# The global part of a joined attention product as eight 64x64 matmuls into free columns of the score banks, with new order lists

## The chip, the cores and the metric

The kernel runs on one core of a Trainium2 chip. The core has a matmul engine (PE; its weight loads are listed apart as PEld), a vector engine (DVE), a scalar engine (ACT), GpSimd (POOL) and a queue that issues transfers (SP). Each engine takes its instructions in the order in which the program lists them, and waits at semaphores for the others. PE writes into PSUM, a memory of eight banks with 512 fp32 columns on each of 128 partitions; DVE and ACT read results from there. The metric is the device time of one launch in microseconds.

## What is computed

Eight batches and eight heads of an attention with a local window, followed by a two-layer network on all 8 x 544 rows:

```python
k_all = concatenate([k_g, k_l]); v_all = concatenate([v_g, v_l])      # 32 global rows, 512 local ones; head size 64
out_g = sm(scale * q_g @ k_all.T) @ v_all                             # global rows see everything
s_ll  = where(abs(i - j) <= 32, scale * q_l @ k_l.T, -1e9)            # a local row sees 32 rows on each side
s_lg  = scale * q_l @ k_g.T                                           # and all 32 global rows
out_l = sm(concatenate([s_lg, s_ll])) @ concatenate([v_g, v_l])
h = x @ w_in                                                          # x: heads side by side, 4352 x 512; w_in 512 x 2048
out = (h * clip(h + 3, 0, 6) / 6) @ w_out                             # w_out 2048 x 512
```

## The kernel before

**A local step.** The 512 local rows of a batch are four blocks of 128, so there are 32 local steps (batch, block), written (b, j). A step sees, for each head, 128 columns of banded local scores and 32 columns of global scores. `local_step` lays out its operations:

- The scores, on PE (line 677, the inner function `pe`): 64x64 tiles of the array, 16 matmuls of 128 columns and 16 of 32 columns. Their result is the tile `scored` (named `s` in the profile): four whole PSUM banks, each with the 160 columns of two heads (columns 0 to 319). There is one such set, the ring "S".
- Eight reductions on DVE (line 703), one a head: mask added, maximum taken, the result written to `sm` in SBUF. When all eight are done the set is given back.
- Eight exponentials on ACT (line 714), then reciprocals and scalings on DVE (lines 725, 730, 736), and a transpose into `et`; from batch 2 on by a transfer (line 759), before that by PE.
- The product with V (`av`, lines 763 to 771): 16 matmuls of 128x64 shape and 64 columns for the local part (line 768), and four of 128x128 shape and 128 columns for the global part (line 771). For the latter `vgz` holds the 32 global rows of V of four heads on 128 partitions, for each pair of heads with zeros where another head's columns stand. The result is one bank, the tile `a`, the ring "A".
- A copy of that result to `xt` in fp16, the network's input (`xa` in `done`, lines 400 on ACT or 402 on DVE, which are the helper `copy`).

**Joined steps.** From the seventh step on (`JOIN = 6`) the scores of a step and the product of the step two before are one operation on PE: `both` issues the scores and then `av` of the older step. There are 26 of these, steps (1,2) to (7,3). Four products before and two at the end run alone (`alone`).

**The global rows.** `global_steps` makes, once a batch, the scores of the 32 global rows of all heads with the same four banks (line 817), two maxima on DVE (832), two exponentials on ACT (840) and scalings (847, 848), a transpose to `eg`, and a product with V into the tile `a` (876).

**The network.** `first` (line 899) multiplies `xt` with a part of `w_in` into one of three banks `m`; ACT makes the clipped part (906) and DVE the product (910) into `gs`. `second` (922) multiplies `gs` with `w_out` in four quarters of four matmuls; ACT or DVE copies the result to `ot` (400, 402), and SP stores it (940). The network of batch b runs among the attention of batch b + 1.

**The order.** All operations are numbered as they are added. `ORDER` holds, for each engine, the list of these numbers in the order in which the engine is to take them; where an operation can go to ACT or DVE (`BOTH`), the list that holds it decides. `Plan.lay` goes through the lists with estimated durations and gives each operation a start and a buffer of its ring; the program is issued over all engines in the order of these starts. At the start 44 idle matmuls are put in between (line 1050). Waits are put in by the framework from the tiles that instructions read and write.

Of the kernel before, what the change touches and what calls it, by code (L numbers as in the profile page):

```python
# [65 lines left out]
    """,  # L66
    "DVE": """
# [242 lines left out]
def kernel(  # L310
# [12 lines left out]
    nc = tc.nc  # L323
    P = 128
# [763 lines left out]
```

## Time and profile before

| | |
|---|---|
| median of 3 runs | 324.29 us (323.80 to 324.64) |
| profiled execution | 324.56 us, of it 322.8 us from its first instruction to its last |
| granted PE clock | 1.0 throughout |
| busy: PE, DVE, ACT, POOL | 312.4, 261.0, 237.8, 121.4 us |
| L922 and L899, the network's products | 126.1 us in 560 matmuls, 119.1 us in 704 |
| L703, the reductions | 68.6 us in 256 |
| L771, the global part | 128 matmuls, 12.7 us busy, the lone steps included |

Rows of the profile name line, engine, operation and tiles as `out<-in`. Matmuls are pipelined: the next starts long before the one ahead has ended, so the cost of a matmul on PE is the distance between starts and not its duration. A merged row of the timeline gives the start of its first instruction and the length up to the end of its last.

### The profile page before, as it was taken

To read this page: it belongs to the slowest core of one execution; us is meant where nothing else is said; L and a number is where in the kernel's file an instruction comes from. 1 tells how busy PE (TensorE), PEld (TensorE's weight loads), DVE (VectorE), ACT (ScalarE), POOL (GpSimd) and SP (SyncE) were. 2 spreads that over 40 slices of the span, in tenths; PEclk is the share of its full clock that TensorE was granted. 3 is DMA by queue.
4 is the path that set the end of the run, shared out by engine and by line. 5 is a ranking of instruction groups with operands and counts; after the bars stand their busy time and mean duration, and the time that the engine had idled before them with its cause. 6 is when DMAs were issued, how large, how long until landed. Compare 5 with 4: busy or idle time off the path is not lost.

```text
span 322.8 us, 9551 instructions
## 1 busy us (share of the span) xinstructions
PE 312.4 (97%) x3554; PEld 178.3 (55%) x3554; DVE 261.0 (81%) x959; ACT 237.8 (74%) x761; POOL 121.4 (38%) x167
## 2 busy tenths in 40 slices
PE   8988999999999999999999999999999999999995
PEld 4557885657855544545444554445444445655443
DVE  4999999899998799789988998889978976476201
ACT  3699999999977897688976897687878834465200
POOL 7958857969190492364334350320000000000000
PEclk9999999999999999999999999999999999999999
DMA  9999999999999999999999999899313055200132
GB/s 162 154 193 172 178 214 156 160 147 150 198 162 201 166 151 171 151 260 183 128 201 215 164 137 179 197 176 206 83 32 68 1 142 156 65 2 0 49 115 99
DMA packets 178863, 46.35 MB, mean 144 GB/s; under 512 B 169344, under 2 KB 173696, under 8 KB 178816
## 3 DMA queue, kind: packets, MB, share of 16 engines
q0 software_dynamic: 108800, 17.28, 76.7%
q1 hardware_dynamic: 70016, 28.45, 44.6%
q8 instruction: 28, 0.46, 0.6%
q14 instruction: 19, 0.16, 0.2%
HBM read 35.65 MB, written 8.91 MB: 138 GB/s over the span
## 4 chain that ended last, share of the span: by engine, by line
PE 73%; DVE 10%; DMA 8%; ACT 6%; issue 2%; SPq 0%; POOLq 0%; DVEq 0%; ACTq 0%
PE m L922 31%; PE m L899 29%; PE s L677 3%; DVE sm L703 3%; PE a L768 3%; PE a L771 3%; DMA eg<-pg 2%; DMA et<-pn 2%; ACT sm L714 2%; DVE gs L910 2%; DVE pn L730 2%; PE a L876 1%; DMA out_dram<-ot 1%; ACT t L906 1%; DMA natg<-in_k_g_dram 1%
## 5 line engine op out<-in xcount | busy, mean ns | idle before, releaser
L922 PE MATMUL m<-wout,gs 128*128 128x512 f16 (+1 forms) x560 | 126.1, 373 | 0.0
L899 PE MATMUL m<-xt,win 128*128 128x512 f16 (+2 forms) x704 | 119.1, 321 | 1.1 <-DVE gs L910 0.4
L714 ACT ACTIVATE sm<-sm,stat 128x160 f32<-128x160 f32 x256 | 107.1, 423 | 12.8 <-DVE stat L703 12.1
L910 DVE SCALAR_TENSOR_TENSOR gs<-t,m 128x512 f16<-128x512 f32 x136 | 91.6, 683 | 18.9 <-ACT t L906 17.9
L899 PEld LDWEIGHTS <-win 128*128 128x128 f16 x768 | 69.0, 98 | 48.4 <-issue 2.8
L906 ACT ACTIVATE t<-m 128x512 f32<-128x512 f32 x136 | 79.4, 595 | 19.7 <-PE m L899 18.4
L922 PEld LDWEIGHTS <-gs 128*128 128x128 f16 x560 | 53.3, 98 | 56.3 <-issue 1.4
L703 DVE CUSTOM_DVE_ANT_0 sm<-s,mask 128x160 f32<-128x160 f32 x256 | 68.6, 317 | 3.7 <-PE s L677 3.5
L714 ACT ACTIVATION_READ_ACCUMULATOR sm<-sm,stat 128x1 f32 x256 | 49.6, 194 | 0.0
L730 DVE TENSOR_TENSOR pn<-sm,stat 128x512 f16<-128x512 f32 x64 | 43.3, 685 | 0.8
L479 POOL DMA_DIRECT2D nat<-in_q_l_dram x30 | 27.3, 918 | 40.8 <-DMA qk<-nat 35.5
L479 POOL DMA_DIRECT2D ve<-in_v_l_dram x40 | 33.1, 839 | 10.8 <-PE a L876 10.8
L400 ACT COPY ot<-m 128x512 f32<-128x512 f32 (+1 forms) x23 | 12.9, 565 | 25.1 <-PE m L922 24.2
L400 ACT CAST xt<-a 128x512 f16<-128x512 f32 x29 | 16.9, 583 | 15.2 <-PE a L771 15.0
L479 POOL DMA_DIRECT2D nat<-in_k_l_dram x30 | 27.3, 913 | 0.4 <-DMA wout<-in_moe_w_out_dram 0.4
L479 POOL DMA_DIRECT2D vgz<-in_v_g_dram x28 | 15.7, 569 | 30.9 <-PE a L771 30.8
L703 DVE DVE_READ_ACCUMULATOR2_ANT stat<- 128x1 f32 x256 | 21.1, 82 | 0.0
L677 PEld LDWEIGHTS <-qk 64*64 64x64 f16 x1024 | 13.5, 107 | 12.5 <-issue 11.2
L402 DVE COPY ot<-m 128x512 f32<-128x512 f32 x12 | 8.2, 686 | 14.6 <-PE m L922 13.2
L677 PE MATMUL s<-qk 64*64 64x128 f16 x512 | 16.6, 224 | 1.1 <-DVE stat L703 0.7
L725 DVE RECIPROCAL stat<-stat 128x4 f32<-128x4 f32 x64 | 10.6, 171 | 6.9 <-ACT sm L714 6.3
L677 PE MATMUL s<-gt,qk 64*64 64x32 f16 x512 | 14.5, 176 | 0.0
(77 smaller groups left out, 253.3 us busy)
## 6 DMA issues: line engine op xcount, KB each, us to landing
out_dram<-ot SPq DMA_DIRECT2D x31, 256.0 KB, 3.7
nat<-in_q_l_dram POOLq DMA_DIRECT2D x30, 128.0 KB, 5.6
nat<-in_k_l_dram POOLq DMA_DIRECT2D x30, 128.0 KB, 5.7
st<-ve SPq DMA_DIRECT2D x14, 256.0 KB, 5.1
ve<-in_v_l_dram POOLq DMA_DIRECT2D x24, 128.0 KB, 5.5
win<-in_moe_w_in_dram POOLq DMA_DIRECT2D x4, 512.0 KB, 9.0
wout<-in_moe_w_out_dram POOLq DMA_DIRECT2D x4, 512.0 KB, 9.7
ve<-in_v_l_dram POOLq DMA_DIRECT2D x8, 96.0 KB, 5.1
```

Of the source, the lines that this page charges most:

```text
L400: nc.scalar.copy(out=out, in_=in_)
L479: nc.gpsimd.dma_start(out=dst(op), in_=src)
L677: nc.tensor.matmul(out=out[q, P:KW] if n == G else out[q, 0:P], lhsT=qk[r][rows, 0, p, UQ + j * P + u * QP:UQ + j * P + (u + 1) * QP], rhs ...
L703: nc.vector.tensor_tensor_reduce(out=sm[sm_op.slot][:, h, :], in0=head(psS[s.slot], h), in1=m, scale=-scale, scalar=3.0e38, op0=ALU.add, o ...
L714: nc.scalar.activation(out=sm[sm_op.slot][:, h, :], in_=sm[sm_op.slot][:, h, :], func=EXP, scale=-1.0, bias=stat[stat_op.slot][:, 0, h:h + 1],
L725: nc.vector.reciprocal(out=stat[stat_op.slot][:, 2, h0:h1], in_=stat[stat_op.slot][:, 1, h0:h1])
L730: nc.vector.tensor_tensor(out=pn[pn_op.slot][:, h0:h1, :], in0=sm[sm_op.slot][:, h0:h1, 0:P], in1=stat[stat_op.slot][:, 2, h0:h1].unsqueez ...
L768: nc.tensor.matmul(out=ps[e * D:(e + 1) * D, h // 2, q], lhsT=x[:, j, h * D:(h + 1) * D], rhs=w[:, h, q], start=u == 0 and h < 2, stop=False)
L899: nc.tensor.matmul(out=psM[op.slot][:, i * n:(i + 1) * n], lhsT=w_in_t[:, m, (c + i) * P:(c + i + 1) * P], rhs=x()[:, m, t0:t0 + n], start ...
L906: nc.scalar.activation(out=t1[to.slot], in_=psM[f.slot], func=RELU, bias=0.5, scale=1.0 / 6.0)
L910: nc.vector.scalar_tensor_tensor(out=gs[set_.slot][:, c:c + k, t0:t0 + n], in0=t1[to.slot].rearrange("f (k t) -> f k t", k=k), scalar=1.0, ...
L922: nc.tensor.matmul(out=psM[(f or op).slot][:, a * n:(a + 1) * n], lhsT=gs[set_.slot][:, c, t0:t0 + P], rhs=w_out_t[:, c, a * n:(a + 1) * n ...
```

## The change

For joined steps alone:

1. The result goes into columns 320 to 447 of the four score banks, in place of the tile `a`: bank p gets the pair of heads p. The joined operation asks for the ring "S" only.
2. The global part comes first, right behind the scores, as eight matmuls on 64 rows, 64 columns of the array and 128 columns of data, one for each head; they use the half of `vgz`'s rows and columns in which the head's values and one other head's zeros stand. They start the sums, and the 16 matmuls of the local part add to them.
3. The copy to `xt` reads the score banks. It depends, beside the product, on the last of the eight reductions that the code adds, `trs[-1]`, which is head 7's. The score banks are given back when all eight reductions and the copy are done.
4. The copy is added after the step's exponentials and no longer before its reductions, so it has another number: in step (4,1) it was 1037 and is 1055, and the reductions of heads 0 to 7, which were 1040, 1042, ... 1054, are 1039, 1041, ... 1053.
5. All five order lists are new. The planner's duration of a joined operation is 955 in place of 1080.

```diff
     "PE": """
...
-        1036 975 954 965 868 1141 966 1137 967 968 1145 1153 1063 1149 1157 1161 1165 1173 1169 1091 1177 1181
...
+        17 14 12 40 65 23 21 61 99 63 90 131 93 95 57 163 124 127 399 391 129 156 195 159 403 407 387 161 235
...
+        1036 954 975 965 868 1141 966 1137 967 1145 968 1153 1063 1149 1157 1161 1165 1173 1169 1177 1181 1091
...
     "ACT": """
...
+        1023 1019 1025 1021 1027 1017 1055 963 1050 1048 1052 956 1040 1046 1054 1142 1143 1044 871 1042 872
...
     "DVE": """
...
+        1029 1018 1028 1032 1030 1033 1031 1034 1037 1038 1053 1047 962 1041 1049 1043 1045 1051 976 1039 977
...
-    psS = [scored]
+    psS, spare_s = [scored], scored[:, :, 2 * KW:2 * KW + P]
...
             def both(op):
                 pe(op)
-                before[0](op.slots[1])
-            s = add("PE", 1080, both, deps + before[1], key=key, acq=("S", "A"), rel=before[2], cols=1664, ins=8 * H + AV)
-            before[3](s)
+                before[0](None)
+            s = add("PE", 955, both, deps + before[1], key=key, acq="S", rel=before[2], cols=1408, ins=8 * H + AV + 8)
...
+        if before:
+            before[3](s, trs[-1:])
+            plan.at = "soft", b, j
...
         def av(slot):
-            ps, w = psA[slot].rearrange("d (p q) -> d p q", p=NP), et[et_op.slot]
+            w = et[et_op.slot]
+            ps = psA[slot].rearrange("d (p q) -> d p q", p=NP) if slot is not None else spare_s
+            if slot is None:
+                for p in range(NP):
+                    for e in range(2):
+                        rows, cols = slice(p % 2 * D, p % 2 * D + D), slice(e * D, e * D + D)
+                        nc.tensor.matmul(out=ps[cols, p, :], lhsT=vgz[r][rows, p, cols], rhs=w[rows, H + p // 2, :],
+                                         start=True, stop=False)
             for u, x in enumerate((ve[b % VE], st[r])):
                 for h in range(H):
                     e, q = h % 2, slice(u * QP, (u + 1) * QP)
                     nc.tensor.matmul(out=ps[e * D:(e + 1) * D, h // 2, q], lhsT=x[:, j, h * D:(h + 1) * D], rhs=w[:, h, q],
-                                     start=u == 0 and h < 2, stop=False)
-            for p in range(NP):
+                                     start=slot is not None and u == 0 and h < 2, stop=slot is None and u == 1)
+            for p in range(NP if slot is not None else 0):
                 nc.tensor.matmul(out=ps[:, p, :], lhsT=vgz[r][:, p, :], rhs=w[:, H + p // 2, :], start=False, stop=p == NP - 1)
...
-        def done(v):
+        def done(v, after=()):
...
             def xa(op):
                 copy(op, xt[xt_op[b].slot][:, :, j * P:(j + 1) * P],
-                     psA[v.slots[-1]].rearrange("k (p q) -> k p q", p=NP))
-            xdone[b, j] = [add(BOTH, (470, 610), xa, [v, xt_op[b]], key=key - 0.5, rel=[v])]
+                     spare_s if after else psA[v.slots[-1]].rearrange("k (p q) -> k p q", p=NP))
+            xdone[b, j] = [add(BOTH, (470, 610), xa, [v, xt_op[b], *after], key=key - 0.5, rel=[v])]
```

179 rows, old and new, of the table ORDER are left out of this document.

## The prediction

> **What bounds the kernel now.** I read the first part of the page, then its chain, then one long window, then the waits.
>
> ```profile
> span 322.8 us, 9551 instructions
> PE 312.4 (97%) x3554; PEld 178.3 (55%) x3554; DVE 261.0 (81%) x959; ACT 237.8 (74%) x761; POOL 121.4 (38%) x167
> ...
> PE 73%; DVE 10%; DMA 8%; ACT 6%; issue 2%; SPq 0%; POOLq 0%; DVEq 0%; ACTq 0%
> PE m L922 31%; PE m L899 29%; PE s L677 3%; DVE sm L703 3%; PE a L768 3%; PE a L771 3%; DMA eg<-pg 2%; DMA et<-pn 2%; ACT sm L714 2%; DVE gs L910 2%; DVE pn L730 2%; PE a L876 1%; DMA out_dram<-ot 1%; ACT t L906 1%; DMA natg<-in_k_g_dram 1%
> ```
>
> The matmul engine is busy nearly all the time, and the chain runs mostly through the two large products (L922, L899). The view of busy time by stretch, for the stretch that holds nearly all joined steps:
>
> ```profile
> core 0: us, PE busy (x) PEld busy (x) DVE busy (x) ACT busy (x) POOL busy (x), PEclk, DMA share, GB/s
> 60.00:265.00 205.00, 203.88 (x2325) 109.05 (x2327) 181.92 (x675) 166.33 (x555) 74.57 (x101) 1.00 1.35 154
> ```
>
> Here PE idles 205.00 - 203.88 = 1.1 us, DVE 23.1 us, ACT 38.7 us, at full clock. So work taken from PE is time won, as long as nothing new makes PE wait. DVE is second: its room is 23 us in 24 of the 26 joined steps, about 0.9 us a step.
>
> **What the change takes away.** In a joined step PE makes the scores (L677), then the local part of an older step's product with V (L768), then its global part (L771). One joined step, step (4,0), in the timeline (start, duration, instruction):
>
> ```profile
> 130.10 0.25 PE L677 MATMUL s<-qk 64*64 64x128 f16 x4
> 130.18 0.19 PE L677 MATMUL s<-gt,qk 64*64 64x32 f16 x4
> 130.21 0.23 PE L677 MATMUL s<-qk 64*64 64x128 f16 x4
> 130.27 0.19 PE L677 MATMUL s<-gt,qk 64*64 64x32 f16 x4
> ...
> 130.44 0.19 PE L677 MATMUL s<-gt,qk 64*64 64x32 f16 x4
> ...
> 130.56 0.32 PE L768 MATMUL a<-et,ve 128*64 128x64 f16 x8
> ...
> 130.70 0.32 DVE L703 CUSTOM_DVE_ANT_0 sm<-s,mask 128x160 f32<-128x160 f32 x1
> 130.71 0.29 PE L768 MATMUL a<-et,st 128*64 128x64 f16 x8
> ...
> 130.94 0.40 PE L771 MATMUL a<-et,vgz 128*128 128x128 f16 x4
> ...
> 131.17 4.48 PE L922 MATMUL m<-wout,gs 128*128 128x512 f16 x20
> ...
> 131.37 0.58 ACT L400 CAST xt<-a 128x512 f16<-128x512 f32 x1 [1.43 <-PE a L771]
> ```
>
> The global part costs 131.17 - 130.94 = 0.23 us. It becomes eight 64x64 matmuls of 128 columns, two rounds of four tiles, in the mode that the scores already use. The second such round of the scores takes 130.27 - 130.21 = 0.06 us, the first 130.18 - 130.10 = 0.08. Two rounds: 0.12 (at worst 0.16); won: 0.11 us a step (0.07). There are three changes of tile shape in a step before and after. The eight weight loads replace four larger ones; the scores do 32 in 0.46 us, 0.014 each, so eight need 0.11 and fit under the two rounds. 26 joined steps: **-2.9 us** (bounds -1.8 and -3.0). Nothing covers this on PE, so all of it counts.
>
> The result no longer needs the bank "a", whose only other users are the few lone products and the global rows' product. In the waits no row has PE waiting for a copy out of "a", so freeing it is worth 0 (at most the 1.1 us that PE idles).
>
> **What the change adds.** The product now lies in free columns of the four score banks, in the tile `s`. Three consequences.
>
> First, a reduction (L703) waits for the last matmul that wrote its tile. In the step above it starts at 130.70, just after the last score row (130.44 + 0.19 = 130.63), with L768 still running into another bank. With L768 writing the same tile it can start when that ends: 130.71 + 0.29 = 131.00, plus 0.12 for the two rounds, plus the same 0.07: 131.19, that is **1.09 us after the step's start in place of 0.60**.
>
> Second, the copy to `xt` reads the same banks as the eight reductions. In the row above the copy on ACT runs at 131.37 beside the reductions on DVE. What happens to two engines that read one tile is shown by the global rows' softmax, batch 6, where DVE takes maxima of `s` (L832) and ACT its exponentials (L840):
>
> ```profile
> 234.47 0.72 DVE L832 TENSOR_REDUCE stat<-s 128x1 f32<-128x544 f32 x1 [0.74 <-PE s L817]
> ...
> 235.23 0.15 DVE L834 TENSOR_SCALAR stat<-stat 128x1 f32<-128x1 f32 x1
> 235.30 0.71 DVE L832 TENSOR_REDUCE stat<-s 128x1 f32<-128x544 f32 x1
> 235.51 0.19 ACT L714 ACTIVATION_READ_ACCUMULATOR sm<-sm,stat 128x1 f32 x1
> ...
> 236.11 0.71 ACT L840 ACTIVATE sg<-s,stat 128x544 f32<-128x544 f32 x1 [0.41 <-DVE stat L832]
> ```
>
> Both order lists put the first half of the heads first (1614 before 1622 on DVE, 1616 before 1624 on ACT). That half's bias is ready at 235.23 + 0.15 = 235.38, ACT is free at 235.70, and yet the exponential starts at 236.11, 0.10 after the second maximum ends (235.30 + 0.71 = 236.01), although that one reads the other half's banks. The waits say the same:
>
> ```profile
> ACT xt L400 <- PE a L771: 15.0, 13, 2.4
> ...
> DVE sm L703 <- PE s L677: 3.5, 4, 1.9
> ...
> ACT sg L840 <- DVE stat L832: 1.8, 3, 1.1
> ...
> PE m L899 <- DVE gs L910: 0.4, 2, 0.2
> ```
>
> So two engines' reads of `s` are taken in turn, in the order in which the program issues them. I apply that to the copy: it waits for the reductions issued before it, and those issued behind it wait for the copy. The Trainium skill, "PSUM — Partial Sum Buffer", section "PSUM bank collisions raise a hardware error", has the reason: two engines on one bank and quadrant at once is an error, reads against reads included, so software must keep them apart. By that rule the copy, which touches all four banks, collides with every reduction; the sum is the same as by the row, and no run here shows an unguarded pair.
>
> The new lists are laid out as if only one reduction mattered. The copy depends in the code on `trs[-1]` alone, head 7's. In step (4,1) the DVE list takes that one first (1053 1047 ... 1041 1049 1043 1045 1051 ... 1039), and the ACT list has the copy, 1055, ahead of the step's first exponential. Of the 26 joined copies 19 stay on ACT; head 7's reduction is first or second of its step in 10 of these and third to sixth in 9. The other 7 are on DVE, where before there was one; the output copies on DVE fall from twelve to nine. Behind the copy in the ACT list stand the step's exponentials (L714). The copies' cost, from the view of the tile `xt` and from the page's groups:
>
> ```profile
> L400 ACT CAST xt<-a x29: 562/585/615, 21.9 to 280.3; 128x512 f16<-128x512 f32 x29
> L402 DVE CAST xt<-a x3: 660/682/685, 27.6 to 270.4; 128x512 f16<-128x512 f32 x3
> ```
> ```profile
> L402 DVE COPY ot<-m 128x512 f32<-128x512 f32 x12 | 8.2, 686 | 14.6 <-PE m L922 13.2 <-DMA out_dram<-ot 1.4
> ```
>
> DVE gets 6 x 0.68 - 3 x 0.69 = +2.0 us of work; and where the copy cuts into the reductions DVE stands still for 0.58 and two hand-overs of about 0.07, **0.72 us**. In some ten steps that is 7 us (bounds: none, 0; all nineteen, 13.7). With the late first reduction (0.49 at most, for the steps where DVE was early, about ten: 4 us) DVE loses 11 + 2 = 13 of its 23 us of room. On average it is no bottleneck, but it works in order, and behind a halted reduction stand L910 and L402, for which PE waits with its three `m` banks. I take a sixth of these 13 us as PE wait, **+2** (bounds 0 and 13), nearest to the row in which PE idles 1.1 us with DVE 89% busy.
>
> Third, the score banks are given back only after the copy. There is one set, so the next score operation on PE waits for it. Three places, steps (4,1), (6,0) and (7,0), where the global scores (L817) follow closest; timeline, start of scores, first and last reduction, next use:
>
> ```profile
> 135.58 0.25 PE L677 MATMUL s<-qk 64*64 64x128 f16 x4
> ...
> 136.53 0.32 DVE L703 CUSTOM_DVE_ANT_0 sm<-s,mask 128x160 f32<-128x160 f32 x1
> ...
> 138.48 0.08 DVE L703 DVE_READ_ACCUMULATOR2_ANT stat<- 128x1 f32 x1
> ...
> 139.48 0.21 PE L817 MATMUL s<-gt 64*32 64x32 f16 x8
> ```
> ```profile
> 230.22 0.25 PE L677 MATMUL s<-qk 64*64 64x128 f16 x4
> ...
> 231.70 0.32 DVE L703 CUSTOM_DVE_ANT_0 sm<-s,mask 128x160 f32<-128x160 f32 x1
> ...
> 233.65 0.08 DVE L703 DVE_READ_ACCUMULATOR2_ANT stat<- 128x1 f32 x1
> ...
> 233.97 0.21 PE L817 MATMUL s<-gt 64*32 64x32 f16 x8
> ```
>
> In both lists the same three quarter products of L922 stand between, so PE arrives 233.97 - 230.22 = 3.75 us after the start, in the new kernel 3.64. Eight reductions in a row take 138.56 - 136.53 = 2.03 us. The new hold is 1.09 + 2.03 + 0.72 + 0.07 = 3.91 if DVE is at hand, and 1.48 + 2.03 + 0.79 = 4.30 if it comes as late as at 231.70: PE waits 0.3 to 0.7, taken 0.45, three times: 1.3 us. Six more crossings have little room in the new PE list: (1,3) to (2,0), (2,1) to global 1, (2,3) to global 2, (5,0) to global 4, (7,2) to global 7, and in (7,1) the first L899 of batch 6, which needs that step's copy and comes behind one quarter product: PE is there after 131.17 - 130.10 - 0.11 = 0.96 and four of the twenty matmuls in 4.48, 0.90, that is 1.86, and the copy cannot end before 1.09 + 0.25 + 0.72 = 2.06. I take 0.3 each, between 0 and the 0.7 above: 1.8 us. Together **+3.1 us** (bounds 0 and 6.3).
>
> The moved entries of the POOL and SP lists add and remove no transfer, and the chain gives both queues 0%: 0. The first four entries of the PE list change places too; the chain has the load of `natg` there with 1% of the span: 0, a microsecond either way. The three output copies given to ACT lie in its 38.7 us of room; 0.
>
> **Sum.** -2.9 + 2.0 + 3.1 = +2.2 us. The profiled execution took 324.56 us (322.8 of span and 1.8 around it), 0.27 above the median of 324.29. 324.56 + 2.2 = 326.8, against the median 326.5; I say **326.6 us**.
>
> **Rivals.**
> - *PE's saving comes through.* DVE's room of 0.9 us a step swallows each halt of 0.72 before PE needs the bank, and the banks come back in time because the new lists put the users of `s` further apart where they could, (5,0) to global 4 by one quarter product. For it: the quoted 23 us of room. Against it: the three crossings above, where the list leaves 3.64 for a hold of 3.91. It decides if PE's waits from `s` and `m` stay under 2 us in all. 324.3 - 2.9 + 0.8 = about 322.2. Chance 0.27.
> - *The waits cancel the saving.* Crossings of 1.3 + 0.9 and a DVE effect under 1: within 0.3% (1 us, about what a measurement of this kernel can tell), 323.3 to 325.3. Chance 0.12.
> - *DVE becomes the bound.* The copy is in turn with the reductions in all nineteen steps and each halt reaches PE by way of the `m` banks: 13.7 + 3.1 - 2.9 = +13.9 at most, with half of it reaching PE +7: 331.3. For it: DVE's 89%. Against it: PE waits for L910 0.4 us in all, by the quoted row. Chance 0.17.
> - *The reads aren't kept in turn.* Then copy and reductions overlap, the hold is 1.09 + 2.03 + 0.07 = 3.2 and fits 3.64. The time is the first rival's, and I count it there; the row at 236.11 speaks against it.
>
> **How the numbers follow.** Likeliest: slower by waits for `s`, 326.6, chance 0.44, own range 325.3 to 329.0. With the DVE case 0.61 slower, 0.12 same, 0.27 faster. The range reaches from 321.5 (the saving whole, no new wait: 324.3 - 2.9) to 331.3.
>
> **What would show it.** In the page after: L771 gone or small, L768 with the 64x64 rows added and PE busy time down by about 3 us. A row "DVE sm L703 <- ACT xt" of some microseconds in the waits and "PE s L817" or "PE s L677 <- ACT xt" of 1 to 4 us. First reductions 1.1 us after a step's start, never 0.6. If copies on ACT run beside reductions on DVE in the timeline, the second consequence is wrong; if the global rounds cost over 0.16 us, the saving is; if PE's idle time from 60 to 265 us stays near 1 us, the kernel is faster and the third is wrong.

## The result and the profile after

The changed kernel takes **328.99 us** (median of 5 runs, 328.48 to 330.12); the kernel before, beside it, 323.97 us (5 runs, 323.80 to 324.64). The ratio is 1.0158, 95% interval 1.0135 to 1.0181: slower, as forecast, and 2.4 us above the 326.6 forecast, inside the range. The change itself was forecast at +2.3 us (326.6 - 324.3) and measured at +5.0, over twice as much. The profiled execution took 328.59 us, 4.0 more than that of before.

The first part of the page after, and its chain:

```profile
span 326.8 us, 9756 instructions
PE 311.0 (95%) x3660; PEld 174.0 (53%) x3660; DVE 261.7 (80%) x959; ACT 237.5 (73%) x761; POOL 121.4 (37%) x167
...
PE 46%; DVE 32%; ACT 11%; DMA 6%; issue 3%; SPq 2%; ACTq 0%; DVEq 0%
```

PE's busy time fell by 1.4 us, and the span rose by 4.0. In the chain DVE's share went from 10% to 32%. Lines have moved: the reductions are L702 now, the exponentials L713, the product's rounds L772 and L777, the global scores L826, the network's products L908 and L931.

The stretch from 60 to 265 us of the changed kernel, in the columns of the view of before (PE, PEld, DVE, ACT, POOL, clock, DMA share, GB/s):

```profile
60.00:265.00 205.00, 198.33 (x2382) 103.17 (x2381) 179.41 (x661) 161.48 (x540) 75.36 (x102) 1.00 1.34 155
```

PE idles 205.00 - 198.33 = 6.7 us in place of 1.1, at full clock, and DVE and ACT are busy for less of it as well: all three engines wait for each other more. The waits of the changed kernel (who waits, for whom, total us, how often, longest):

```profile
ACT xt L400 <- DVE stat L702: 13.8, 12, 2.7
DVE sm L702 <- ACT xt L400: 9.4, 16, 0.7
...
PE m L908 <- DVE gs L919: 2.2, 7, 0.7
...
PE s L826 <- DVE stat L702: 1.8, 4, 0.7
DVE sm L702 <- PE s L777: 1.6, 3, 0.8
PE s L677 <- DVE stat L702: 1.2, 4, 0.4
```

The first two rows are new: the copy on ACT waits 13.8 us for reductions on DVE, and the reductions 9.4 us for the copy. Not all of the 13.8 is added waiting: before, ACT's copies to `xt` waited 15.0 us for the product (a row that the prediction shows). Step (4,1), for which the prediction worked out the hold of the banks, in the timeline:

```profile
136.38 0.25 PE L677 MATMUL s<-qk 64*64 64x128 f16 x4
...
136.76 0.28 PE L772 MATMUL s<-et,vgz 64*64 64x128 f16 x8
136.97 0.32 PE L777 MATMUL s<-et,ve 128*64 128x64 f16 x8
...
137.34 2.92 PE L931 MATMUL m<-wout,gs 128*128 128x512 f16 x12
137.46 0.32 DVE L702 CUSTOM_DVE_ANT_0 sm<-s,mask 128x160 f32<-128x160 f32 x1
...
137.95 0.08 DVE L702 DVE_READ_ACCUMULATOR2_ANT stat<- 128x1 f32 x1
138.12 0.59 ACT L400 CAST xt<-s 128x512 f16<-128x512 f32 x1 [2.40 <-DVE stat L702]
...
138.74 0.33 DVE L702 CUSTOM_DVE_ANT_0 sm<-s,mask 128x160 f32<-128x160 f32 x1 [0.71 <-ACT xt L400]
...
140.21 0.08 DVE L702 DVE_READ_ACCUMULATOR2_ANT stat<- 128x1 f32 x1
...
140.35 0.21 PE L826 MATMUL s<-gt 64*32 64x32 f16 x8
```

The joined operation now lasts 137.34 - 136.38 = 0.96 us instead of 1.07. The first reduction comes 1.08 us after the start. Two reductions run, the copy waits for them, the third waits for the copy: it starts 0.79 us later than its place at 137.95. The banks come back at 140.21 + 0.08 = 140.29, 3.91 after the start, and the next user of `s` starts at 140.35.

Where PE's time went is seen in its groups (busy, mean ns of one, idle just before). First before, then after:

```profile
L899 PE MATMUL m<-xt,win 128*128 128x512 f16 (+2 forms) x704 | 119.1, 321 | 1.1 <-DVE gs L910 0.4 <-DVE xt L402 0.3 <-DVE ot L402 0.2
L677 PE MATMUL s<-qk 64*64 64x128 f16 x512 | 16.6, 224 | 1.1 <-DVE stat L703 0.7 <-ACT sg L840 0.2
L817 PE MATMUL s<-gt 64*32 64x32 f16 x64 | 1.7, 186 | 0.2 <-DVE stat L703 0.2
```
```profile
L908 PE MATMUL m<-xt,win 128*128 128x512 f16 (+2 forms) x704 | 121.1, 321 | 3.7 <-DVE gs L919 2.2 <-ACT xt L400 0.6 <-ACT et L400 0.4
L677 PE MATMUL s<-qk 64*64 64x128 f16 x512 | 16.6, 224 | 1.7 <-DVE stat L702 1.2 <-DVE qk L402 0.4
L826 PE MATMUL s<-gt 64*32 64x32 f16 x64 | 1.7, 186 | 1.9 <-DVE stat L702 1.8
```

Idle time before the matmuls into `s` grew from 1.1 + 0.2 to 1.7 + 1.9, by 2.3 us (0.4 of it after is for `qk` and not for the banks). The network's first product waits 3.7 instead of 1.1, and its matmuls, each as long as before (321 ns), cover 121.1 us instead of 119.1: they overlap less. That is 4.6 us. With the 2.9 us saved (26 x 0.11) the sum is -2.9 + 2.3 + 4.6 = +4.0, the whole difference of the spans; the small changes of the other groups cancel. The saving shows in the groups of the product too: all its matmuls, lone steps included, cover 32.3 us before and 29.5 after.

### The profile page after: what moved, and what is told of

The parts are those of the page before. It is cut to its first block, busy times and chain, and to the rows that moved or that the text cites. A ratio compares the mean times of both kernels' runs of the same rounds, so it can differ in the third digit from the quotient of the medians.

```text
span 326.8 us, 9756 instructions
## 1 busy us (share of the span) xinstructions
PE 311.0 (95%) x3660; PEld 174.0 (53%) x3660; DVE 261.7 (80%) x959; ACT 237.5 (73%) x761; POOL 121.4 (37%) x167
## 4 chain that ended last, share of the span: by engine, by line
PE 46%; DVE 32%; ACT 11%; DMA 6%; issue 3%; SPq 2%; ACTq 0%; DVEq 0%
PE m L931 20%; PE m L908 19%; DVE sm L702 10%; DVE gs L919 8%; DVE pn L732 5%; ACT sm L713 5%; DMA et<-pn 3%; ACT xt L400 2%; ACT t L915 2%; PE s L677 2%; DMA out_dram<-ot 2%; PE s L777 1%; DVE pn L738 1%; DMA single<-in_q_l_dram 1%; DVE et L402 1%
## 5 line engine op out<-in xcount | busy, mean ns | idle before, releaser
L931 PE MATMUL m<-wout,gs 128*128 128x512 f16 (+1 forms) x560 | 126.2, 373 | 0.0
L908 PE MATMUL m<-xt,win 128*128 128x512 f16 (+2 forms) x704 | 121.1, 321 | 3.7 <-DVE gs L919 2.2
L713 ACT ACTIVATE sm<-sm,stat 128x160 f32<-128x160 f32 x256 | 107.1, 421 | 15.5 <-DVE stat L702 15.4
L908 PEld LDWEIGHTS <-win 128*128 128x128 f16 x768 | 68.2, 98 | 53.0 <-issue 6.2
L931 PEld LDWEIGHTS <-gs 128*128 128x128 f16 x560 | 52.9, 98 | 56.9 <-issue 1.5
L702 DVE CUSTOM_DVE_ANT_0 sm<-s,mask 128x160 f32<-128x160 f32 x256 | 70.2, 319 | 11.6 <-ACT xt L400 9.4
L713 ACT ACTIVATION_READ_ACCUMULATOR sm<-sm,stat 128x1 f32 x256 | 49.1, 192 | 0.0
L400 ACT COPY ot<-m 128x512 f32<-128x512 f32 (+1 forms) x26 | 14.3, 569 | 23.6 <-PE m L931 22.4
L702 DVE DVE_READ_ACCUMULATOR2_ANT stat<- 128x1 f32 x256 | 21.2, 83 | 0.0
L400 ACT CAST xt<-s 128x512 f16<-128x512 f32 x19 | 11.1, 582 | 13.9 <-DVE stat L702 13.8
L677 PEld LDWEIGHTS <-qk 64*64 64x64 f16 x1024 | 13.5, 107 | 13.7 <-issue 11.3
L402 DVE COPY ot<-m 128x512 f32<-128x512 f32 x9 | 6.2, 686 | 17.6 <-DMA out_dram<-ot 10.6
L738 DVE TENSOR_TENSOR pn<-sm,stat 128x256 f16<-128x256 f32 x32 | 13.4, 420 | 0.1
```

The source lines that it names most:

```text
L400: nc.scalar.copy(out=out, in_=in_)
L402: nc.vector.tensor_copy(out=out, in_=in_)
L677: nc.tensor.matmul(out=out[q, P:KW] if n == G else out[q, 0:P], lhsT=qk[r][rows, 0, p, UQ + j * P + u * QP:UQ + j * P + (u + 1) * QP], rhs ...
L702: nc.vector.tensor_tensor_reduce(out=sm[sm_op.slot][:, h, :], in0=head(psS[s.slot], h), in1=m, scale=-scale, scalar=3.0e38, op0=ALU.add, o ...
L713: nc.scalar.activation(out=sm[sm_op.slot][:, h, :], in_=sm[sm_op.slot][:, h, :], func=EXP, scale=-1.0, bias=stat[stat_op.slot][:, 0, h:h + 1],
L738: nc.vector.tensor_tensor(out=pn[pn_op.slot][:, H:H + 2, :].rearrange("q a (h g) -> q (a h) g", g=G), in0=sm[sm_op.slot][:, :, P:KW], in1= ...
```

## The experiments

The theory was: the 64x64 form saves what was forecast, and the loss comes from one thing only, that the copy and the reductions read one tile and are taken in turn, which halts both engines and holds the banks. The rivals: that the late first reduction costs the time; that holding the banks does, with or without turns; that the new lists are poor by themselves; that the chip keeps two readers apart whatever the program says.

**New lists, copy from bank `a`.** The changed kernel without the turns; the copy finds old contents.

```diff
-                     spare_s if after else psA[v.slots[-1]].rearrange("k (p q) -> k p q", p=NP))
+                     psA[0 if after else v.slots[-1]].rearrange("k (p q) -> k p q", p=NP))
```

> The changed kernel with one edit: in joined steps the copy to xt reads the bank a, where old contents lie, and no longer the score banks (so the network gets other rows; all else is computed). The 64x64 rounds, the product in the score banks, the late first reduction and the new lists stay; the turns between copy and reductions and the longer hold of the score banks go. If those two are what costs (my theory), the saving of 2.9 us on PE is left: 321 to 323.5 us. If the new lists cost by themselves, it stays at 327 or more. If the late first reduction is the cost, 326 or more.

Measured: 0.9923 of before (0.9884 to 0.9963). The row "DVE sm <- ACT xt" is gone, and PE idles 2.5 us in the stretch instead of 6.7:

```profile
60.00:265.00 205.00, 202.53 (x2464) 106.43 (x2463) 183.48 (x685) 163.06 (x551) 74.50 (x101) 1.00 1.34 155
```

What the copy reads is the whole difference between faster than before and slower: 2.35%, 7.6 us. One thing more goes with it: old contents of `a` are ready at any time, so in joined steps the copy waits for no product either, for which ACT waited 15.0 us before. The runs with two tiles below, which wait for the product and leave nothing out, show that this alone doesn't explain the difference.

**Old lists, copy from bank `a`.** The same on the lists of the kernel before, so that form and lists come apart.

```diff
...
+                for p in range(NP):
+                    for e in range(2):
+                        rows, cols = slice(p % 2 * D, p % 2 * D + D), slice(e * D, e * D + D)
+                        nc.tensor.matmul(out=ps[cols, p, :], lhsT=vgz[r][rows, p, cols], ..., start=True, stop=False)
...
                 copy(op, xt[...], psA[v.slots[-1]].rearrange("k (p q) -> k p q", p=NP))
...
```

> The kernel before with its own lists and planner, the joined product made as in the change (64x64 rounds, in the score banks), the copy reading the bank a (old contents, so the network gets other rows). Theory: the saving alone, and a little lost to the later first reduction: 321 to 323 us. If the later first reduction is the cost, 326 or more. If the new lists are the cost, about 322 here too, and only the run with the new lists is slow.

Measured: 0.9913 (0.9878 to 0.9947). Without the turns, new and old lists take the same time within these intervals.

**Old lists, old form, copy from bank `a`.** The global part stays four 128x128 matmuls behind the local part; only its place is new, so that reductions start late.

```diff
...
-            ps = psA[slot].rearrange("d (p q) -> d p q", p=NP)
+            ps = psA[slot].rearrange("d (p q) -> d p q", p=NP) if slot is not None else spare_s
...
```

> As the run with the old lists, but the global part stays four 128x128 matmuls behind the local part; only the place of the result is new, so the first reduction comes late (about 1.2 us after the step's start) and nothing is saved on PE. The copy reads the bank a (old contents). Theory: the late first reduction costs 0 to 1 us: 324 to 325. Rival, late reductions are the cost: 327 or more. The run with the 64x64 rounds should be faster than this one by 26 x 0.11 = 2.9 us (1.8 to 3.2).

Measured: 1.0015 (0.9989 to 1.0042). Its waits show reductions that wait for the product, and the time shows no cost beyond its interval (at most 0.4%):

```profile
DVE sm L703 <- PE s L772: 7.7, 8, 2.6
```

As the copy from `a` spares ACT its wait for the product, a small cost could hide behind that. Against the run before it the 64x64 form is worth 1.0015 - 0.9913 = 1.0%, 3.3 us, just over the 1.8 to 3.2 expected; the intervals of both ratios, 0.3% each, leave room for the 2.9. The product's matmuls cover 32.3 us here and 29.5 there.

**Old lists, copy from `s`.** The whole change of form, place and copy on the lists of before: the edit of "Old lists, copy from bank `a`", but with this line.

```diff
...
-                     psA[v.slots[-1]].rearrange("k (p q) -> k p q", p=NP))
+                     spare_s if joined else psA[v.slots[-1]].rearrange("k (p q) -> k p q", p=NP))
...
```

> The whole change of product, place and copy, on the old lists and the old planner: the copy reads the score banks and is issued mostly ahead of the step's reductions, which then wait for it. Theory (turns and hold cost): slower than the run with the copy from a by 5 to 12 us, 327 to 334. Rival (the new lists are the cost): as fast as with the copy from a, 321 to 324.

Measured: 1.0077 (1.0039 to 1.0114), so 1.64% more than with the copy from `a`, 5.3 us, near the lower end of what was expected. Its waits, and the groups of PE to hold against those of the changed kernel above:

```profile
ACT xt L400 <- PE s L775: 10.9, 10, 2.1
DVE sm L703 <- ACT xt L400: 9.4, 16, 1.3
...
ACT xt L400 <- DVE stat L703: 1.7, 4, 1.1
```
```profile
L906 PE MATMUL m<-xt,win 128*128 128x512 f16 (+2 forms) x704 | 120.2, 321 | 2.8 <-DVE gs L917 1.7 <-DVE xt L402 0.3 <-DVE ot L402 0.2
L677 PE MATMUL s<-qk 64*64 64x128 f16 x512 | 16.7, 224 | 1.1 <-DVE stat L703 0.7 <-ACT qk L400 0.2 <-ACT sg L847 0.2
L824 PE MATMUL s<-gt 64*32 64x32 f16 x64 | 1.7, 186 | 0.7 <-DVE stat L703 0.5
```

DVE is halted as much as in the changed kernel, but ACT's copies hardly wait for reductions; they wait for the product, as before the change. The old lists issue most copies ahead of all eight reductions, the new ones in their middle or behind. The new lists cost 1.0158 - 1.0077 = 0.8% more (2.6 us), and as far as can be told only where turns are taken. PE's groups show where: against this run the first product loses (3.7 - 2.8) + (121.1 - 120.2) = 1.8 us more in the changed kernel, and the matmuls into `s` wait (1.7 + 1.9) - (1.1 + 0.7) = 1.8 us more. Smaller groups give some of it back, as the spans differ by 326.8 - 324.8 = 2.0.

**Old lists, old form, copy from `s`.** The place and the copy alone: four 128x128 matmuls into `s`, as two runs ago, and the copy reads them there.

```diff
...
-                     psA[v.slots[-1]].rearrange("k (p q) -> k p q", p=NP))
+                     spare_s if joined else psA[v.slots[-1]].rearrange("k (p q) -> k p q", p=NP))
```

> Lists of the kernel before, one tile of score banks; the global part as before in four 128x128 matmuls behind the local part, but the result in the free columns of the score banks and copied from there: the cost of the place alone, without the saving. Nothing is left out. My theory, saving and place add up: the run with both took 1.0077 of before, the saving alone measured 0.0102, so 1.018, 330 us (328.5 to 331.5), PE busy between 60 and 265 us up by the saving, its idle time as in that run. Rival, the saved PE time is only turned into waiting in that kernel (PE waits for the banks anyway): the time is that of the run with both, 326.8 us (326 to 328).

Measured: 1.0167 (1.0130 to 1.0205), 329.73 us. The saving is worth 1.0167 - 1.0077 = 0.9%, 2.9 us, here too: it is not turned into waiting, it is won beside whatever the turns cost.

**Old lists, two tiles.** The four banks become two tiles of two banks. In each step the last head of either parity to be reduced shares a tile with the product; the other six have the first tile.

```diff
-    scored = pp.tile([P, 4, 512], FP32, tag="s", name="s")
-    psS = [scored]
+    scored = [pp.tile([P, 2, 512], FP32, tag="s" + x, name="s" + x) for x in "xy"]
+    psS, spare_s = [scored], scored[1][:, :, KW:KW + 2 * P]
...
+            i = sorted(range(h % 2, H, 2), key=lambda x: trs[x].start).index(h)
+            return ps[1][:, h % 2, 0:KW] if i == 3 else ps[0][:, h % 2, i * KW:(i + 1) * KW]
...
+                    copy(op, out.rearrange("k (a c) q -> k a c q", c=2), spare_s.rearrange("k c (a q) -> k a c q", a=2))
...
```

> The four score banks become two tiles of two banks each: one holds the six heads whose reductions come first in the order of the step, the other the last two heads and the product with V (two pairs of heads to a bank, 256 columns behind a head's 160). Lists of the kernel before, global part in 64x64 rounds, the copy reads the product, so the whole of the computation is done. My theory, that copy and reductions are kept apart because they read one tile, and that this and nothing else of the change costs time: the first reductions start at 0.6 us again, no row 'DVE sm <- ACT xt' above 1 us, and the time is that of the run with the copy from bank a on these lists, 0.991 of before: 321.3 us (319.5 to 322.5). Rival, the cost is that of holding the banks until the copy, whatever the tiles: the banks still come back after the copy and two reductions, so the time stays near the 1.008 of the run with one tile, 326.8 us (325.5 to 328). Rival, the chip keeps reads by two engines apart by itself, whatever the tile: then reductions still pause beside the copy, 325 us or more.

Measured: **0.9926** (0.9900 to 0.9953), 322.16 us: faster than both kernels, with the whole computation done. Its stretch, its waits between copy, product and reductions, and step (4,1) in its timeline:

```profile
60.00:265.00 205.00, 203.77 (x2470) 107.31 (x2469) 183.12 (x683) 166.01 (x555) 76.75 (x104) 1.00 1.33 158
```
```profile
ACT xt L400 <- PE sy L776: 13.5, 13, 2.5
...
DVE sm L703 <- ACT xt L400: 0.8, 2, 0.4
```
```profile
135.52 0.24 PE L677 MATMUL sx<-qk 64*64 64x128 f16 x2
...
136.61 0.32 DVE L703 CUSTOM_DVE_ANT_0 sm<-sx,mask 128x160 f32<-128x160 f32 x1
136.71 0.58 ACT L400 CAST xt<-sy 128x512 f16<-128x512 f32 x1 [1.53 <-PE sy L776]
136.85 0.08 DVE L703 DVE_READ_ACCUMULATOR2_ANT stat<- 128x1 f32 x1
136.85 0.32 DVE L703 CUSTOM_DVE_ANT_0 sm<-sx,mask 128x160 f32<-128x160 f32 x1
...
138.07 0.32 DVE L703 CUSTOM_DVE_ANT_0 sm<-sy,mask 128x160 f32<-128x160 f32 x1
...
138.32 0.09 DVE L703 DVE_READ_ACCUMULATOR2_ANT stat<- 128x1 f32 x1
```

PE idles 1.2 us, as before the change. The copy waits for the product as it did before (13.5 us in 13 waits), and the reductions hardly wait for it. The copy of `sy` runs beside reductions of `sx` at 0.24 us apart, the pace they have without a copy, and by the time the reductions of `sy` come it has ended. The banks come back at 138.41, 2.89 us after the start, where the changed kernel has 3.91 and the kernel before 138.56 - 135.58 = 2.98: without the turns the copy falls within the time of the reductions. The rival in the form on record, that waiting for the copy costs whatever the tiles, falls: it put the time at 326.8 us. That the turns lengthen the hold is a part of their cost, though, and this run takes it away together with the halts and the late first reduction: what a long hold would cost without turns stays open. Two engines that read different banks both go on (0.58 us for the copy, 0.24 between reductions); whether the chip would keep readers of one bank apart was not tested. The Trainium skill, "PSUM — Partial Sum Buffer", section "PSUM bank collisions raise a hardware error", counts collisions by bank and by group of 32 partitions and says that different banks run clean; by that rule the first six reductions need no order with the copy, and this timeline agrees, by the same two numbers.

**New lists, two tiles.** The changed kernel, with the same two tiles and nothing else.

```diff
-    scored = pp.tile([P, 4, 512], FP32, tag="s", name="s")
-    psS, spare_s = [scored], scored[:, :, 2 * KW:2 * KW + P]
+    scored = [pp.tile([P, 2, 512], FP32, tag="s" + x, name="s" + x) for x in "xy"]
+    psS, spare_s = [scored], scored[1][:, :, KW:KW + 2 * P]
...
```

> The changed kernel with its own lists, score banks as two tiles as in the run beside it; nothing is left out. In 13 of its 26 joined steps the copy is issued ahead of both reductions of its tile, in 13 behind one or both. My theory, the lists cost nothing without the turns and some of the turns stay where the copy is issued last: between the 0.992 of this list with the copy from bank a and 1.000: 322 to 324.3 us, taken 322.5. Rival, the new lists are poor by themselves once the copy reads what it has to read: 326 us or more.

Measured: 0.9948 (0.9921 to 0.9976), 323.00 us. The same lists with one tile: 1.0158. What is left of the turns is small, as these lists issue some copies late:

```profile
DVE sm L702 <- ACT xt L400: 2.5, 6, 0.7
```

**The kernel before, two tiles.** Product and copy as before; only the tiles differ.

```diff
...
-            at = scored[:, 2 * e:2 * e + 2, :].rearrange("q a c -> q (a c)")[:, 512 - G:1024]
+            at = scored[e].rearrange("q a c -> q (a c)")[:, 512 - G:1024]
...
```

> The kernel before, with nothing changed but the score banks as two tiles; product with V as before in bank a. This asks the row on which the prediction's second consequence rests: in the global rows' softmax the first exponential started 0.10 us after the second half's maximum ended. If turns are by tile, the exponential of the first half now starts when its own bias is there, some 0.6 us earlier, beside the second half's maximum; the time is the same or a little better, 323 to 324.4 us (ratio 0.997 to 1.001). If the exponential waited for something else (ACT's own list, the banks), it starts as late as before.

Measured: 1.0002 (0.9969 to 1.0036): the tiles by themselves are worth nothing that can be told. The global rows' softmax of batch 6 in its timeline, the place on which the prediction rested:

```profile
233.34 0.19 PE L817 MATMUL sx<-gt 64*32 64x32 f16 x1
...
234.60 0.15 DVE L834 TENSOR_SCALAR stat<-stat 128x1 f32<-128x1 f32 x1
234.67 0.71 DVE L832 TENSOR_REDUCE stat<-sy 128x1 f32<-128x544 f32 x1
...
234.99 0.69 ACT L840 ACTIVATE sg<-sx,stat 128x544 f32<-128x544 f32 x1
```

The exponential of the first half starts at 234.99, when ACT is free, beside the second half's maximum (234.67 to 235.38). With one tile it waited for that maximum's end, 2.14 us after the scores' start (236.11 - 233.97); here 234.99 - 233.34 = 1.65, 0.49 earlier (some 0.6 was expected). The two halves lie in different banks in both kernels, so the order was set by the tile, not by the banks.

**A short read in the copy's place.** New lists, one tile, copy from `a`, but a read of one column of `s` ahead of it.

```diff
...
+                if after:
+                    copy(op, crumb[op.eng], spare_s[:, 0, 0:1])
                 copy(op, xt[xt_op[b].slot][:, :, j * P:(j + 1) * P],
-                     spare_s if after else psA[v.slots[-1]].rearrange("k (p q) -> k p q", p=NP))
+                     psA[0 if after else v.slots[-1]].rearrange("k (p q) -> k p q", p=NP))
```

> The changed kernel with its own lists and one tile, where the copy of a joined step reads bank a (old contents, so the rows of the network are other ones, as in the first run of this kind), but is preceded on its engine by a read of one column of the score tile, 128x1. The turn is taken in the same place, but the read is short: 128x1 pieces take 0.08 to 0.2 us in the traces, the copy 0.58. Theory, the cost follows the time for which the turn is held (DVE's halts of 0.79 fall to about 0.4, the banks come back about 0.4 earlier): of the 2.35% between the two runs on these lists half is left, 1.003 to 1.006 of before, 325.6 us (324.8 to 326.3). Rival, what costs is that the order between the two engines is fixed at all: ACT's 13.8 us of waiting for the reductions issued before, with the exponentials behind it, stays whole; then 1.011 to 1.016, 328 to 329 us. Rival, only long reads matter: under 1.000.

Measured: 1.0052 (1.0021 to 1.0082), as a ratio inside the 1.003 to 1.006 that the theory expected. The waits:

```profile
ACT crumbACT L401 <- DVE stat L703: 14.2, 12, 2.8
...
DVE sm L703 <- ACT crumbACT L401: 2.8, 10, 0.3
```

DVE's halts fell from 9.4 to 2.8 us, ACT's waits stayed at 14, and a little over half of the loss stayed too (1.0052 - 0.9923 = 1.29 of 2.35%). So the length of the turn counts, and so does a fixed order with short turns. Two prices can be fitted to two pairs of runs: 9.4 and 1.7 us of halts of DVE and ACT cost 1.64% (old lists), 9.4 and 13.8 us 2.35% (new lists). That makes 0.059% for one us of ACT's waiting (0.71 / 12.1) and 0.164% for one of DVE's, 0.19 and 0.53 us of the kernel's time. For the short read they give 2.8 x 0.164 + 14.2 x 0.059 = 1.30%, where 1.29 was measured. With intervals of 0.3 to 0.4% on each ratio so close an agreement is partly luck: for the old form with the copy from `s` they give 10.9 x 0.164 + 1.8 x 0.059 = 1.89%, where 1.0167 - 1.0015 = 1.52 was measured.

The second price isn't that of ACT's waiting as such. Before the change ACT's copies waited 15.0 us, and with old lists and two tiles 13.5, both for the product; PE idles only 1.1 and 1.2 us there. Whether it stands for the exponentials queued behind a copy that waits for reductions, or for the longer wait for the score banks that the groups of PE show on the new lists, no run separates.

**The copy twice.** The changed kernel with each joined copy issued twice.

```diff
-                copy(op, xt[xt_op[b].slot][:, :, j * P:(j + 1) * P],
+                for _ in range(2 if after else 1):
+                    copy(op, xt[xt_op[b].slot][:, :, j * P:(j + 1) * P],
...
```

> The changed kernel with each joined copy issued twice in a row; the second writes the same again, nothing is left out. ACT and DVE get 19 and 7 copies more, 11 and 5 us, and each turn lasts 0.58 longer. Theory, the cost follows the time for which the turn is held: the turns now cost 7.6 us on these lists with halts of 0.79 us; with 1.37 they cost 7.6 x 1.37 / 0.79 = 13.2, so 5.6 us more: 334.6 us (332.5 to 337). Rival, the cost is that of the order being fixed: 0 to 2 us more, 329 to 331.

Measured: 1.0518 (1.0457 to 1.0580), 342.45 us: above both expectations. Its stretch and its waits:

```profile
60.00:265.00 205.00, 187.20 (x2244) 97.36 (x2242) 173.50 (x640) 160.75 (x524) 73.87 (x100) 1.00 1.28 152
```
```profile
DVE sm L702 <- ACT xt L400: 20.0, 18, 1.3
...
ACT xt L400 <- DVE stat L702: 15.8, 13, 3.5
...
PE s L827 <- DVE stat L702: 6.3, 5, 1.7
PE m L909 <- DVE gs L920: 5.4, 9, 1.1
```

By the two prices it would have lost 20.0 x 0.164 + 15.8 x 0.059 = 4.2% against the copy from `a`; it lost 1.0518 - 0.9923 = 5.95%. The theory had the direction and about half of the step (5.6 us expected, 11.7 measured by the ratios). The loss grows faster than the time for which a turn is held; that the slack of the lists is used up by then would explain it, but no run separates that from the copies' own time on the engines.

All together, in order of what DVE's halts add up to, with PE's idle time from 60 to 265 us worked out from each run's row of that view, halts from its waits:

| kernel | DVE for the copy, us | ACT's copy for DVE, us | PE idle, us | ratio |
|---|---|---|---|---|
| before | 0 | 0 | 1.1 | 1 |
| before, two tiles | 0 | 0 | 1.2 | 1.0002 |
| old lists, old form, copy from `a` | 0 | 0 | 1.0 | 1.0015 |
| old lists, copy from `a` | 0 | 0 | 1.4 | 0.9913 |
| new lists, copy from `a` | 0 | 0 | 2.5 | 0.9923 |
| old lists, two tiles | 0.8 | 0 | 1.2 | 0.9926 |
| new lists, two tiles | 2.5 | 0 | 1.0 | 0.9948 |
| new lists, short read of `s` | 2.8 | 14.2 | 4.8 | 1.0052 |
| old lists, copy from `s` | 9.4 | 1.7 | 3.9 | 1.0077 |
| new lists, copy from `s` (the change) | 9.4 | 13.8 | 6.7 | 1.0158 |
| old lists, old form, copy from `s` | 10.9 | 1.8 | 4.1 | 1.0167 |
| new lists, copy twice | 20.0 | 15.8 | 17.8 | 1.0518 |

## Why the prediction was right, point by point

The direction and the mechanism, reads of one tile taken in turn, were right. The size was less so: +2.2 us in the sum, +4.0 between the profiled spans. One term was too low by 2.6 us and another too high by 0.8, and that the time still lies in the range owes something to a range 10 us wide.

- **The saving, -2.9 us (0.11 a step): right.** The joined operation went from 1.07 to 0.96 us, two pairs of runs that differ in the form alone give 3.3 and 2.9 us, and the product's matmuls cover 2.8 us less.
- **First reductions at 1.09 us in place of 0.60: right (1.08 in step (4,1)), and free as far as can be told.** I had let them take 4 of DVE's 23 us of room; the run with late reductions is not clearly slower than before, though its copy has no wait for the product.
- **Reads of one tile are taken in turn: right.** The same softmax with two tiles shows the exponential beside the maximum, and with two tiles the change is faster than before. The reason that the prediction gave, two engines on one bank, isn't the one at work in its row: the two halves there lie in different banks, and the order goes by the tile.
- **A halt of 0.72 us in some ten steps, 7 us: near.** One halt is 0.79 in step (4,1); 16 waits make 9.4 us, 0.59 each.
- **"I take a sixth of these 13 us as PE wait, +2": the term that was mis-sized.** The network's first product shows +4.6 us, 2.6 idle and 2.0 in matmuls that overlap less. The sixth was a guess. On the old lists, with the same 9.4 us of halts of DVE, the product shows (2.8 - 1.1) + (120.2 - 119.1) = +2.8; the other 1.8 come with the new lists, where the copy stands among the reductions. I had counted DVE's loss alone. The new order also makes the copy on ACT wait for reductions, with the step's exponentials queued behind it; the text named that queue and gave it no price. It is the likely reading of the 1.8 us, and not shown: before, ACT's copies waited as long for the product, and the wait for the score banks is longer with the new lists as well.
- **Waits for `s`, +3.1 us: a little high.** The hold in (4,1) is 3.91 us as worked out, and PE's idle time before `s` grew by 2.3 us.
- **DVE's extra copies, +2.0 us of work, and three output copies moved to ACT:** not tested apart; DVE's busy time rose by 0.7 us only.
- **The rivals.** "The saving comes through" needed waits from `s` and `m` under 2 us in all; they grew by 2.3 + 2.6, with 2.0 of lost overlap beside them. It is what two tiles bring: 322.2 was forecast for that case, and 322.16 measured on the old lists, 323.00 on the new ones; that the first agrees to a tenth is luck. "The waits cancel the saving" fell with the ratio (1.0135 to 1.0181). "The reads aren't kept in turn" fell with the timeline. "DVE becomes the bound" is not this kernel, though the copy issued twice shows where it begins.

## What to carry to other kernels

A free corner of a buffer is not free if another engine still reads that buffer: ask which reads become ordered, how long each turn is held, where in the order the new reader stands, and what is queued behind both engines, even where both have room on average. If the saving is real (here 2.9 and 3.3 us in two pairings), move the border of the tile before giving it up: two tiles of two banks, with the readers that come last beside the new result, turned a loss of 1.6% into a gain of 0.5% on the new lists, and one of 0.8% into a gain of 0.7% on the old ones.

## What the runs showed that was not expected

- The same waiting can cost nothing or much: ACT waits 15.0 us at these copies before the change and 13.8 in the changed kernel; what differs is what it waits for.
- Waits on PE cost more than their idle time in the groups: the first product's 704 matmuls kept their mean of 321 ns, yet covered 2.0 us more, beside 2.6 us of idle time. That each restart leaves a matmul without a neighbour to overlap with is the likely reading; it was not measured by itself.
- Lists that can't be told apart in time (0.9923 and 0.9913) differ by 0.8% once the same copy has to take turns.
- The loss is not in proportion: some 0.58 us more in each turn, from the second copy, more than doubled it (2.35% to 5.95%).
